# Packed attention and SwiGLU on one core: early packed weights at their final scale in PSUM, and a new order of all engines

## The chip, the cores and the metric

The kernel runs on 1 core of one Trainium2 chip. The metric is the device time of one execution in microseconds (us); the time of the kernel before is the median of 3 runs. A profile is one execution taken by the hardware profiler. Its engines are PE (TensorE, matmuls), PEld (its weight loads), DVE (VectorE), ACT (ScalarE), POOL (GpSimd) and SP (SyncE, which here issues all transfers).

## The reference

```python
# q, k, v: (8, 8, 576, 64); p: (8, 8, 32, 64); scale = 1 / sqrt(64)
def sm_attn(qq, kk, vv):
    s = scale * np.matmul(qq, kk.transpose(0, 1, 3, 2))
    s = s - np.max(s, axis=-1, keepdims=True)
    a = np.exp(s)
    a = a / (np.sum(a, axis=-1, keepdims=True) + 1e-09)
    return np.matmul(a, vv)
p_packed = sm_attn(p, k, v)              # 32 packed rows per head
out = sm_attn(q, p_packed, p_packed)
# x: (4608, 512), the heads side by side; d_ff = 1536
xn = x / np.sqrt(np.mean(x * x, axis=-1, keepdims=True) + 1e-06) * rms_g
g = xn @ w_gate
return (g / (1 + np.exp(-g)) * (xn @ w_val)) @ w_out
```

The three weights arrive as 64-bit floating point numbers, as pairs of 32-bit words.

## The kernel before

**What is computed, and in which pieces.** The second attention multiplies its weights `a` with the packed rows, and the result goes through `w_gate` and `w_val`. The kernel therefore multiplies the packed rows with these weights once per batch ("packed weights", `packed_weights`, L1138): for each of 6 column groups `c` a matmul group on the fp32 weights `wgv` (L1172) into two PSUM banks, which `pw_evict` (L1212) splits into two fp16 parts in `ring`. From batch 3 on (`PW16_FROM`) the weights have themselves been split into fp16 (`weights16`, L1192) and the matmuls are those of L1184. The tokens go through in 12 units of 384 (`u`). For each there is `query` (loading and transposing q), `attention` (scores L1357 or L1364, softmax, norm, and the attention transposed in `aTu`) and the MLP: the up projection, 24 groups of L1549, with `gated` (SiLU, product, split into two fp16 parts in `hall`), and the down projection, three outputs of 36 matmuls each (L1574), with `store`. `keysets` and `stage1` do the first attention of a batch. Units 0 and 1 and batches 0 and 1 ("early") work in fp32 on PE.

**The front.** The 12 pieces of `w_gate` and `w_val` (`gv_piece`, L581) and 6 of `w_out` (`wo_piece`) are 1 MB each and go through nine raw rooms that are used again. `to_f32` (L540) makes fp32 of them: ACT takes the high halves (L548); the low halves go by a letter of `LOW` or `LOW_WO`: "D" two DVE operations (L563, L565), "A" one of ACT (L558) and one of DVE (L560), "P" one of POOL (L553) and one of DVE (L555). A norm of each pair of pieces (L618 on PE, reduced over 512 columns at L623) gives its scale `gv_r` and the value half's factor `ratio` (L631). When all norms are there, `wo_split` splits `w_out` (ACT L707, DVE L709, and a copy by ACT, L715, or POOL, L712, by a letter of `WO_HI`); the down projection of unit 0 needs it.

**Scales.** In batches 0 to 2 the gate half is multiplied with `pg` itself and the value half with `pg` times `ratio` (L1157, L1159; the engine by `PGV_BY`); the eviction then scales by the column `gv_r`:

```python
yield from split(hi, lo, ps[e], pw_sc[:, c : c + 1] if b < PW16_FROM else 2.0**-14, 512, t0, DVE)
```

`split` is an ACT activation with a scale (L513) and a DVE `scalar_tensor_tensor` (L515), which takes the high part away.

**What sets the order.** The functions are generators that ask a planner (`Plan`) for a room or for an engine with a cost in us. The planner runs them against its own clock and writes the order of every engine's queue, which the chip then follows. Which step goes first is set by `RANK`, `BUMP`, `LATER`, `CHOICE` and `AGE`, tables with one entry per phase; `SLACK` holds PE steps outside the MLP back; `KEYS_AFTER` says behind which weight load the keys of batch 1 are let go. Letters as in `KEYS_BY`, `QUERY_BY`, `A1T_BY`, `H_HI` and `H_LO` name the engine that copies. Where PE would wait in the front, `fill` puts in matmuls on constants ("fillers", L1656, 256 columns).

Of the kernel before, what the change touches and what calls it, by code (L numbers as in the profile page):

```python
# [18 lines left out]
P = 128  # L19
# [15 lines left out]
LATENCY = {PE: 0.299, ACT: 0.177, EXP: 0.177, SILU: 0.177, DVE: 0.14, DVE2: 0.14, POOL: 0.005}  # L35
# [12 lines left out]
AGE = (0.106, 0.001, 0.011, 0.097, 0.0, 0.0, 0.486)  # L48
# [5 lines left out]
WINDOW, DENSE = 3.41, 0.47  # L54

# [36 lines left out]
class Plan:  # L92
# [104 lines left out]
    def start(self, chain):  # L197
        kind, _, *at = chain.ask[:3]
        e = ENGINE[kind]
        if at and at[0] is not None:  # L200
# [4 lines left out]
        t = float(ready)
        if e == "pe" and chain.key[0] != "mlp":
            t += SLACK[self.phase]
        free = self.free[e] + (TABLE if kind in (EXP, SILU) and kind != self.table else 0.0)
        return max(free, t), ready
# [18 lines left out]

    def fill(self, until, matmul):

        begin = self.free["pe"]
        if self.stage or until > FILL[2] or until - begin < FILL[0]:
            return
        spare = [(r[0], n, name) for name in ("pm", "psc") for n, r in enumerate(self.rooms[name])]
        if len(self.rooms["pa"]) == 2:
            spare.append((max(r[0] for r in self.rooms["pa"]), 0, "pa"))
        spare = [x for x in spare if x[0] <= max(0.0, begin - FILL[4])]
        unit = 0.213 if self.slow(begin) else 0.125
# [8 lines left out]
        self.free["pe"] += unit * count  # L247
        self.rooms[name][n] = (t, room)

    def run(self, matmul):  # L250
        while self.chains:
            self.settle()
            steps = [c for c in self.chains if c.ask is not None and c.ask[0] in ENGINE]
            if not steps:
                assert not self.chains, [(c.key, c.ask) for c in self.chains]
                return
            starts = []
            for c in steps:
                t, ready = self.start(c)
                t -= AGE[self.phase] * max(0.0, t - ready)  # L260
                starts.append((t, self.precedence(c), c))
            first = min(starts, key=lambda s: s[:2])
            e = ENGINE[first[2].ask[0]]
            window = CHOICE[self.phase][e]
            chain = min(
                (s for s in starts if ENGINE[s[2].ask[0]] == e and s[0] <= first[0] + window), key=lambda s: (s[1], s[0])
            )[2]
            t, ready = self.start(chain)
            kind, cost, *_ = chain.ask
            if e == "pe":  # L270
                self.fill(t, matmul)
                t = max(t, self.free["pe"])
            if kind == LOAD:
                self.free[e] = t + 0.45
                self.landed = max(self.landed, t + LOADING[0]) + cost / LOADING[1]
                seen = self.landed + LOADING[2]
            elif kind == TPOSE:
                issue = 0.1 + cost / 786432 * 3.5
                self.free[e] = t + issue
                self.landed = max(self.landed + 0.9 * issue, t + issue)  # L280
                seen = self.landed + TURNING
            else:
                if kind in (EXP, SILU) and kind != self.table:
# [17 lines left out]
RANK = ({'attention': 0.0, 'conv': 34.24, 'g': 13.88, 'gated': 0.0, 'keys': 0.0, 'mlp': 1000000000.0, 'pw': 7.98, 'pw_evict': 8.66, 'query': 0.0, 'scales': 15.65, 'stage1': 2.05, 'store': 16.88, 'v': 9.6, 'w': 23.15, 'wo': 10.17, 'wo_split': 40.04}, {'attention': 81.35, 'conv': 17.08, 'g': 20.02, 'gated': 9.94, 'keys': 8.3, 'mlp': 1000000000.0, 'pw': 3.23, 'pw_evict': 1.17, 'query': 5.95, 'scales': 4.48, 'stage1': 17.4, 'store': 12.51, 'v': 30.41, 'w': 10.59, 'wo': 4.57, 'wo_split': 14.41}, {'attention': 23.62, 'conv': 32.67, 'g': 28.29, 'gated': 0.0, 'keys': 14.43, 'mlp': 1000000000.0, 'pw': 4.11, 'pw_evict': 3.27, 'query': 4.57, 'scales': 3.23, 'stage1': 0.0, 'store': 0.0, 'v': 7.35, 'w': 31.34, 'wo': 21.47, 'wo_split': 11.2}, {'attention': 22.8, 'conv': 8.01, 'g': 30.57, 'gated': 0.0, 'keys': 0.0, 'mlp': 1000000000.0, 'pw': 6.0, 'pw_evict': 7.89, 'query': 9.74, 'scales': 0.0, 'stage1': 10.65, 'store': 22.96, 'v': 14.82, 'w': 0.37, 'wo': 2.3, 'wo_split': 14.0}, {'attention': 25.03, 'conv': 2.72, 'g': 6.23, 'gated': 5.32, 'keys': 18.98, 'mlp': 1000000000.0, 'pw': 21.74, 'pw_evict': 1.05, 'query': 10.61, 'scales': 5.16, 'stage1': 24.79, 'store': 4.96, 'v': 8.99, 'w': 9.01, 'wo': 1.31, 'wo_split': 6.69}, {'attention': 17.8, 'conv': 0.0, 'g': 7.83, 'gated': 8.05, 'keys': 15.4, 'mlp': 1000000000.0, 'pw': 0.0, 'pw_evict': 3.38, 'query': 27.04, 'scales': 4.68, 'stage1': 19.89, 'store': 10.11, 'v': 56.26, 'w': 22.66, 'wo': 18.33, 'wo_split': 0.0}, {'attention': 0.59, 'conv': 16.59, 'g': 22.57, 'gated': 10.43, 'keys': 46.12, 'mlp': 1000000000.0, 'pw': 5.64, 'pw_evict': 0.0, 'query': 16.98, 'scales': 26.73, 'stage1': 34.01, 'store': 6.52, 'v': 23.39, 'w': 15.29, 'wo': 27.47, 'wo_split': 7.09})  # L301
# [13 lines left out]
KV_LOAD = (1.05, 0.95)  # L315
# [1393 lines left out]
```

## Time and profile before

| what | value |
| --- | --- |
| median of 3 runs | 752.8 us (751.02 to 755.01) |
| profiled execution | 753.8 us; span from first to last instruction 751.7 us |
| PE, DVE, ACT, POOL busy | 727.1, 484.5, 461.6, 124.0 us |
| mean granted clock of PE | 0.99 of full |
| transfers | 82.31 MB |

A busy PE also holds its fillers and matmuls at a lower granted clock, so its 97% is not useful work alone. Idle time of an engine that sets nothing costs nothing.

### The profile page before, as it was taken

To read this page: it belongs to the slowest core of one execution; us is meant where nothing else is said; L and a number is where in the kernel's file an instruction comes from. 1 tells how busy PE (TensorE), PEld (TensorE's weight loads), DVE (VectorE), ACT (ScalarE), POOL (GpSimd) and SP (SyncE) were. 2 spreads that over 40 slices of the span, in tenths; PEclk is the share of its full clock that TensorE was granted. 3 is DMA by queue.
4 is the path that set the end of the run, shared out by engine and by line. 5 is a ranking of instruction groups with operands and counts; after the bars stand their busy time and mean duration, and the time that the engine had idled before them with its cause. 6 is when DMAs were issued, how large, how long until landed. Compare 5 with 4: busy or idle time off the path is not lost.

```text
span 751.7 us, 20141 instructions
## 1 busy us (share of the span) xinstructions
PE 727.1 (97%) x8537; PEld 439.8 (59%) x8537; DVE 484.5 (64%) x1084; ACT 461.6 (61%) x959; POOL 124.0 (17%) x138
## 2 busy tenths in 40 slices
PE   8889999999999999999999999999989999999997
PEld 6765655875555554585555464685544464684553
DVE  4899797875896886777576555586447463572330
ACT  3597796886787676586387376587366274371330
POOL 1213230020342242121011011010001011010010
PEclk9899999999999999999999999999999999999999
DMA  8998413355366165424724923363321213301001
GB/s 291 386 313 303 152 33 79 77 143 140 81 142 133 45 149 150 75 64 80 175 66 79 204 68 104 80 122 102 90 43 23 71 37 98 72 3 43 21 1 43
DMA packets 131418, 82.31 MB, mean 109 GB/s; under 512 B 98432, under 2 KB 110720, under 8 KB 131328
## 3 DMA queue, kind: packets, MB, share of 16 engines
q1 hardware_dynamic: 131328, 81.02, 41.5%
q8 instruction: 67, 1.10, 0.6%
q14 instruction: 23, 0.19, 0.1%
HBM read 47.97 MB, written 9.44 MB: 76 GB/s over the span
## 4 chain that ended last, share of the span: by engine, by line
PE 79%; DMA 6%; ACT 6%; DVE 5%; issue 2%; SPq 1%; POOL 0%; ACTq 0%; DVEq 0%; POOLq 0%
PE pm_2x L1574 10%; PE pm_0x L1574 9%; PE pm_1x L1549 9%; PE pm_2x L1549 9%; PE pm_1x L1574 8%; PE pm_3x L1549 8%; PE pm_3x L1574 7%; PE pm_0x L1549 7%; DMA ring<-in_moe_w_val_dram 2%; DMA wo<-in_moe_w_val_dram 2%; PE psa L1364 2%; PE psb L1017 2%; PE pm_3x L1184 1%; DMA big_1x<-big_5x 1%; PE psa L923 1%
## 5 line engine op out<-in xcount | busy, mean ns | idle before, releaser
L1549 PEld LDWEIGHTS <-ring 128*128 128x128 f16 x2304 | 204.9, 98 | 91.9 <-issue 20.6
L1574 PEld LDWEIGHTS <-hall 128*128 128x128 f16 x1296 | 123.4, 98 | 149.3 <-issue 9.0
L1574 PE MATMUL pm_2x<-wo,hall 128*128 128x512 f16 x360 | 81.4, 379 | 2.1 <-ACT wo L715 1.2
L1603 POOL TENSOR_TENSOR hall<-t_0x,hall 128x384 f16<-128x384 f32 x36 | 36.3, 1007 | 285.0 <-ACT hall L1600 275.7
L1574 PE MATMUL pm_0x<-wo,hall 128*128 128x512 f16 x360 | 81.0, 379 | 0.0
L1574 PE MATMUL pm_3x<-wo,hall 128*128 128x512 f16 x288 | 65.9, 379 | 0.0
L1574 PE MATMUL pm_1x<-wo,hall 128*128 128x512 f16 x288 | 64.5, 379 | 0.0
L1600 ACT CAST hall<-t_1x 128x384 f16<-128x384 f32 x71 | 36.2, 509 | 26.5 <-DVE t_1x L1586 26.1
L1603 POOL TENSOR_TENSOR hall<-t_1x,hall 128x384 f16<-128x384 f32 x29 | 28.9, 998 | 134.2 <-ACT hall L1600 125.7
L1549 PE MATMUL pm_3x<-aTu_0x,ring 128*128 128x192 f16 (+1 forms) x330 | 45.8, 282 | 1.5 <-DVE ring L515 1.2
L1549 PE MATMUL pm_1x<-aTu_0x,ring 128*128 128x384 f16 (+1 forms) x306 | 45.4, 292 | 0.4 <-DVE ring L515 0.4
L1549 PE MATMUL pm_2x<-aTu_1x,ring 128*128 128x192 f16 (+1 forms) x324 | 45.8, 285 | 0.0
L1549 PE MATMUL pm_1x<-aTu_1x,ring 128*128 128x192 f16 (+1 forms) x330 | 44.7, 279 | 0.9 <-ACT t_0x L1583 0.8
L1600 ACT CAST hall<-t_0x 128x384 f16<-128x384 f32 x67 | 34.1, 509 | 17.4 <-DVE t_0x L1586 17.1
L1549 PE MATMUL pm_2x<-aTu_0x,ring 128*128 128x192 f16 (+1 forms) x288 | 41.1, 287 | 0.7 <-ACT t_1x L1583 0.6
L1549 PE MATMUL pm_3x<-aTu_1x,ring 128*128 128x384 f16 (+1 forms) x258 | 37.7, 289 | 0.0
L1549 PE MATMUL pm_0x<-aTu_1x,ring 128*128 128x384 f16 (+1 forms) x240 | 36.6, 294 | 0.0
L1549 PE MATMUL pm_0x<-aTu_0x,ring 128*128 128x384 f16 (+1 forms) x228 | 34.3, 292 | 1.0 <-DVE ring L515 0.5
L1606 DVE TENSOR_TENSOR hall<-t_1x,hall 128x384 f16<-128x384 f32 x44 | 24.5, 557 | 6.6 <-ACT hall L1600 5.9
L1583 ACT ACT_TABLE_LOAD x15 | 19.2, 1283 | 8.9 <-PE pm_1x L1549 5.3
L1583 ACT ACTIVATE t_0x<-pm_0x,usc_1x 128x384 f32<-128x384 f32 x14 | 8.1, 579 | 26.8 <-PE pm_0x L1549 26.7
L1606 DVE TENSOR_TENSOR hall<-t_0x,hall 128x384 f16<-128x384 f32 x35 | 20.8, 594 | 5.2 <-ACT hall L1600 5.0
(972 smaller groups left out, 1405.8 us busy)
## 6 DMA issues: line engine op xcount, KB each, us to landing
out_dram<-o_1x SPq DMA_DIRECT2D x19, 256.0 KB, 2.0
out_dram<-o_0x SPq DMA_DIRECT2D x17, 256.0 KB, 2.2
hall<-in_moe_w_out_dram SPq DMA_DIRECT2D x4, 1024.0 KB, 6.5
wo<-in_moe_w_gate_dram SPq DMA_DIRECT2D x3, 1024.0 KB, 15.3
wo<-in_moe_w_val_dram SPq DMA_DIRECT2D x3, 1024.0 KB, 13.5
big_2x<-in_k_dram SPq DMA_DIRECT2D x5, 576.0 KB, 5.5
big_1x<-in_q_dram SPq DMA_DIRECT2D x3, 768.0 KB, 6.0
ring<-in_moe_w_gate_dram SPq DMA_DIRECT2D x2, 1024.0 KB, 13.2
```

The costliest lines, as they stand in the source:

```text
L923: nc.tensor.matmul(flat[r, KP * c0 : KP * c1], pT[:, 2 * g + hl, r], kTs[j // 2][1][:, n + c0 : n + c1, q], start=(hl == 0), stop=(hl == 1),)
L1017: nc.tensor.matmul(pps[g][32 * j : 32 * j + 32, :D], a1T[h, c, 32 * j : 32 * j + 32], half(vf0[b, j // 2])[h, j % 2, order[c], :], start=( ...
L1184: nc.tensor.matmul(ps[e][32 * j : 32 * j + 32, :], pg[h, lp, j, :], wgv16[h, c, j, lw, :], start=(n3 == 0), stop=(n3 == 2),)
L1364: nc.tensor.matmul(ps2[o : o + n, i, :, pi, :], qT[:, lq, i, pi, o : o + n], packs[b][3][:, lp, pi, :, :], start=(j == 0), stop=(j == 2),)
L1549: nc.tensor.matmul(psi[:, :, o : o + n], pw[:, g, lw, w, f * P : (f + 1) * P], aT[:, :, la, g, o : o + n], start=(j == 0), stop=(j == 5),)
L1574: nc.tensor.matmul(po, hall[:, ft, lh, ts], wo[:, ft, 1 - lw, :], start=(n == 0), stop=(n == 3 * NFT - 1))
L1583: nc.scalar.activation(t, pss[0][:, :UT], AF.Silu, scale=sc[:, c, 0:1])
L1600: nc.scalar.copy(hall[:, ft, 0, :], t)
L1603: nc.gpsimd.tensor_tensor(hall[:, ft, 1, :], t, hall[:, ft, 0, :], ALU.subtract)
L1606: nc.vector.tensor_tensor(hall[:, ft, 1, :], t, hall[:, ft, 0, :], ALU.subtract)
```

## The change

Four edits change what is computed where, and one the order of everything:

1. `packed_weights` of batches 0 to 2 multiplies `pg` with both columns of `gv_r` before the matmuls (two ACT activations, or one DVE or POOL operation over 256 columns), and the eviction scales by the constant 1.0. `ratio` and `vg_sc` go.
2. The norm of a pair of weights adds both column halves in one PSUM range; L623 reduces 256 columns.
3. Four small operations of `load_g` go from DVE to POOL. Fillers have 512 columns.
4. The letters that name engines are new, and `KEYS_AFTER` is 10.
5. The planner charges PE for a change between matmuls on part of the array and on the whole (`SWITCH`) and for the fetch of PE's instructions, counted by the matmul (`FETCH`); costs, ranks and the other tables are new. Branches for splitting in other ways are added, which the letters chosen (`LO_BY`, `SPLIT_BY`, `MUL_BY`) leave unused.

The core of the diff:

```diff
-SLACK = (0.04, 0.166, 0.039, 0.236, 0.337, 0.234, 0.47)
+SLACK = (0.081, 0.203, 0.691, 0.758, 0.387, 0.765, 0.246)
+SWITCH = 0.093
+FETCH = (4.3, 6.3, 8.0)
+FETCH_AT, FETCH_NEED, FETCH_SIZE = 128, 449, 256
...
+    def fetched(self, t, cost, n):
+        a, b = self.count, self.count + 2 * n
+        self.count = b
+        late = 0.0
+        for k in range(max(0, (a - FETCH_NEED) // FETCH_SIZE), b // FETCH_SIZE + 1):
+            for at in (FETCH_SIZE * k + FETCH_AT, FETCH_SIZE * (k - 1) + FETCH_NEED):
+                if not a <= at < b:
+                    continue
+                x = t + late + cost * (at - a) / (b - a)
+                if at == FETCH_SIZE * k + FETCH_AT:
+                    self.avail[k] = x + FETCH[0 if self.landed <= x else 2 if self.stage == 0 and x < 90 else 1]
+                else:
+                    late += max(0.0, self.avail.get(k - 1, 0.0) - x)
+        return cost + late
...
-A1T_BY = "DAADAD"
+A1T_BY = "DDDDAD"
-PGV_BY = "DAPAAA"
-GM_BY = "ADDADD"
-LOW = "DDPDDDAAADDA"
-LOW_WO = "DPAPDP"
-KEYS_AFTER = 13
-KEYS_BY = "DDDAAADDDAAD"
-QUERY_BY = "DDADAA"
-H_HI = "DDAADAADADAD"
-H_LO = "PDPDPPPDDPDP"
-H_LO_MIXED = "DDDDDPDPDPPD"
-H_LO_ONE = "PPDDDDPDPPPD"
+PGV_BY = "DAPAAP"
+GM_BY = "AADADA"
+LOW = "ADPAAAADAPAP"
+LOW_WO = "APAPDP"
+KEYS_AFTER = 10
+KEYS_BY = "DAADADDDDADA"
+QUERY_BY = "AAADDA"
+H_HI = "DADDDAADDDAD"
+H_LO = "DPDDPDDPDPPP"
+H_LO_MIXED = "DPDPPDPDPDDD"
+H_LO_ONE = "PDPDPPPPPDDD"
-GV_BY = "PPDDPP"
-WO_HI = "AAPPAP"
+GV_BY = "PDDDPP"
+WO_HI = "AAAAAP"
...
-                        pn[:, (2 * w + f) * P : (2 * w + f + 1) * P], r, r, start=(kt == 0), stop=(kt == NKT - 1)
+                        pn[:, w * P : (w + 1) * P], r, r, start=(f + kt == 0), stop=(f == 1 and kt == NKT - 1)
-        nc.vector.tensor_reduce(mx, pn.rearrange("p (w f) -> p w f", w=2), AX.X, ALU.max)
+        nc.vector.tensor_reduce(mx, pn[:, : 2 * P].rearrange("p (w f) -> p w f", w=2), AX.X, ALU.max)
-        nc.vector.tensor_scalar(ratio[:, c : c + 1], u[:, 0:1], s[:, 1:2], 0.5, ALU.mult, ALU.mult)
...
-                    nc.scalar.activation(pgs[1], pg, AF.Copy, scale=ratio[:, c : c + 1])
+                    for w in range(2):
+                        nc.scalar.activation(pgs[:, w], pg, AF.Copy, scale=gv_r[:, c, w : w + 1])
                 else:
-                    (nc.vector if by == "D" else nc.gpsimd).tensor_scalar_mul(pgs[1], pg, ratio[:, c : c + 1])
+                    (nc.vector if by == "D" else nc.gpsimd).tensor_tensor(
+                        pgs.rearrange("p w j r -> p w (j r)"),
+                        pg.rearrange("p j r -> p (j r)").unsqueeze(1).broadcast_to([P, 2, P]),
+                        gv_r[:, c].unsqueeze(2).broadcast_to([P, 2, P]), ALU.mult,
+                    )
...
-            yield from split(hi, lo, ps[e], pw_sc[:, c : c + 1] if b < PW16_FROM else 2.0**-14, 512, t0, DVE)
+                yield from split(hi, lo, ps[e], 1.0 if b < PW16_FROM else 2.0**-14, 512, t0, DVE)
...
-        nc.tensor.matmul(room[:, 0, :256] if len(room.shape) == 3 else room[:, :256], margin, fill, start=True, stop=True)
+        nc.tensor.matmul(room[:, 0, :512] if len(room.shape) == 3 else room[:, :512], margin, fill, start=True, stop=True)
```

## Rows read from the trace of the kernel before

**Rows 1.** Windows: length, busy us of each engine, clock, DMA share, GB/s.

```profile
20.00:54.00 34.00, 28.35 (x326) 21.79 (x323) 31.60 (x67) 25.07 (x45) 6.95 (x9) 0.85 1.06 344
54.00:110.00 56.00, 51.83 (x684) 33.97 (x684) 50.25 (x100) 46.16 (x76) 18.29 (x19) 1.00 0.52 181
110.00:160.00 50.00, 49.69 (x745) 34.29 (x744) 39.81 (x94) 36.84 (x86) 4.99 (x6) 1.00 0.40 92
160.00:735.00 575.00, 566.89 (x6416) 330.50 (x6414) 353.10 (x799) 345.76 (x741) 90.99 (x90) 1.00 0.37 86
735.00:752.00 17.00, 12.76 (x60) 5.59 (x57) 1.24 (x2) 0.47 (x1) 0.00 (x0) 0.95 0.08 32
```

**Rows 2.** The chain that ended last, the front: start, us, what.

```profile
7.17 14.12 DMA ring<-in_moe_w_val_dram
...
22.97 5.10 PE psa L1357 x24
...
40.67 13.49 DMA wo<-in_moe_w_val_dram
...
103.07 1.24 POOL wo L712
...
108.47 1.05 ACT wo L715
...
109.56 2.53 PE pm_2x L1574 x11
```

**Rows 3.** Waits of PE: who waited for whom, total us, times, longest.

```profile
PE psa L1441 <- issue: 2.1, 1, 2.1
PE psa L1357 <- DVE misc L1056: 2.1, 1, 2.1
...
PE pm_2x L1574 <- ACT wo L715: 1.2, 1, 1.2
...
PE psa L923 <- DMA big_5x<-big_1x: 1.0, 1, 1.0
PE pm_2x L1574 <- issue: 0.9, 1, 0.9
...
PE psa L1364 <- DMA big_1x<-big_5x: 0.8, 1, 0.8
```

**Rows 4.** PE alone while L1357 ran: window, busy, clock, DMA share, GB/s.

```profile
23.00:28.00 5.00, 5.00 (x26) 0.53 1.05 386
```

**Rows 5.** Timeline of DVE: start, us, line, operation, tiles.

```profile
30.56 0.68 DVE L623 TENSOR_REDUCE tiny_11x<-pm_3x 128x2 f32<-128x512 f32 x1
31.16 0.69 DVE L563 TENSOR_SCALAR wgv<-wgv 128x1024 uint32<-128x1024 uint32 x1
...
34.76 0.21 DVE L631 TENSOR_SCALAR ratio<-tiny_12x,gv_r 128x1 f32<-128x1 f32 x1
34.89 1.22 DVE L565 SCALAR_TENSOR_TENSOR wgv<-wo,wgv 128x1024 uint32<-128x1024 uint32 x1
...
37.95 0.42 DVE L1252 TENSOR_SCALAR aT_0x<-psb 128x256 f32<-128x256 f32 x1
38.29 1.22 DVE L565 SCALAR_TENSOR_TENSOR wgv<-wo,wgv 128x1024 uint32<-128x1024 uint32 x1
```

**Rows 6.** Evictions into `ring`, ACT and DVE: count, ns min/median/max, starts, form.

```profile
L513 ACT ACTIVATE ring<-pm_0x x19: 577/592/602, 249.4 to 670.8; 128x512 f16<-128x512 f32 x19
...
L513 ACT ACTIVATE ring<-pm_0x,gv_r x7: 663/680/706, 66.2 to 208.2; 128x512 f16<-128x512 f32 x7
...
L515 DVE SCALAR_TENSOR_TENSOR ring<-pm_0x,ring x19: 680/682/692, 250.1 to 671.4; 128x512 f16<-128x512 f32 x19
...
L515 DVE SCALAR_TENSOR_TENSOR ring<-pm_1x,gv_r,ring x11: 736/743/751, 40.6 to 221.7; 128x512 f16<-128x512 f32 x11
```

**Rows 7.** Two ACT operations of the front, columns as in rows 6.

```profile
L558 ACT ACTIVATE hall<-hall x3: 1123/1146/1199, 38.6 to 65.1; 128x1024 uint32<-128x1024 uint8 x3
...
L1157 ACT ACTIVATE pgh_1x<-pg_0x,ratio x3: 398/401/402, 46.2 to 72.1; 128x128 f32<-128x128 f32 x3
```

More of the change, by code (lines that the diff above doesn't have):

```diff
@@ L26 @@
 DVE2 = "dve2"
+PET = "pet"
 EXP, SILU = "exp", "silu"
-ENGINE = {PE: "pe", ACT: "act", EXP: "act", SILU: "act", DVE: "dve", DVE2: "dve", POOL: "pool", LOAD: "sp", TPOSE: "sp"}
+ENGINE = {PE: "pe", PET: "pe", ACT: "act", EXP: "act", SILU: "act", DVE: "dve", DVE2: "dve", POOL: "pool", LOAD: "sp", TPOSE: "sp"}
 ENGINES = (
@@ L208, in start @@
         free = self.free[e] + (TABLE if kind in (EXP, SILU) and kind != self.table else 0.0)
+        if kind == PET and not self.tiled:
+            free += SWITCH
         return max(free, t), ready
@@ L237, in fill @@
         spare = [x for x in spare if x[0] <= max(0.0, begin - FILL[4])]
-        unit = 0.213 if self.slow(begin) else 0.125
+        unit = 0.42 if self.slow(begin) else 0.232
         count = int((FILL[1] * (until - begin) - FILL[3]) / unit)
@@ L246, in fill @@
         self.work.append((begin, begin + unit * count, 1.0))
-        self.free["pe"] += unit * count
+        self.free["pe"] += self.fetched(begin, unit * count, count)
+        self.tiled = False
         self.rooms[name][n] = (t, room)
@@ L307 @@
+LATER = {'attention': 78.44, 'conv': -63.68, 'g': -131.85, 'gated': 45.4, 'keys': 72.7, 'pw': 1.66, 'pw_evict': -105.25, 'query': 18.16, 'scales': -18.72, 'stage1': -12.53, 'store': 16.97, 'v': 32.7, 'w': 23.17, 'wo': -135.91, 'wo_split': 125.94}
 RAW_AT = (0, 1, 2, 3, 4, 5, 6, 7, 8, 4, 5, 6)
@@ L409, in upper @@
         return x.bitcast(BF16)[..., 1::2]
-    misc = cpool.tile([P, 640], F32, name="misc")
-    fill = misc[:, 512:640].bitcast(BF16)
+    misc = cpool.tile([P, 768], F32, name="misc")
+    fill = misc[:, 512:768].bitcast(BF16)
     nc.gpsimd.memset(fill, 0.0)
+    minus = fill.bitcast(F16)[:, :P]
+    nc.gpsimd.tensor_scalar_mul(minus, ident, -1.0)
     neghalf = cpool.tile([P, 1], F32, name="neghalf")
@@ L430, in tile_packed_attention_then_swiglu @@
     gv_r = cpool.tile([P, NFC, 2], F32, name="gv_r")
-    pw_sc = gv_r[:, :, 0]
-    ratio = cpool.tile([P, NFC], F32, name="ratio")
-    vg_sc = cpool.tile([P, NFC], F32, name="vg_sc")
     wo_sc = cpool.tile([P, NFC], F32, name="wo_sc")
@@ L703, in wo_split @@
         x, sc = wo32[:, 2 * i : 2 * i + 2, :], wo_sc[:, i : i + 1]
+        if SPLIT_BY[i] == "H":
+            for f in range(2):
+                st = yield Room("o")
+                k = 2 * i + f
+                hi, lo = wo[:, k, 1, :], wo[:, k, 0, :]
+                yield (ACT, act(512) + 0.03) if SPLIT_ST[k] == "A" else (DVE2, 0.37)
+                if SPLIT_ST[k] == "A":
+                    nc.scalar.activation(st, wo32[:, k], AF.Copy, scale=sc)
+                else:
+                    nc.vector.tensor_scalar_mul(st, wo32[:, k], sc)
+                yield (ACT, act(512)) if HALF_HI[k] == "A" else (DVE, 0.34)
+                (nc.scalar.copy if HALF_HI[k] == "A" else nc.vector.tensor_copy)(hi, st)
+                if SPLIT_LO[k] == "P":
+                    yield POOL, 1.17
+                    nc.gpsimd.tensor_tensor(lo, st, hi, ALU.subtract)
+                else:
+                    yield DVE2, dve(512) + 0.1
+                    nc.vector.tensor_tensor(lo, st, hi, ALU.subtract)
+                plan.give("o", st)
+            plan.mark("wo_hl", i)
+            return
         hi0 = yield Room("o")
         hi = hi0.bitcast(F16).rearrange("p (f n) -> p f n", f=2)
-        yield ACT, act(1024)
+        yield ACT, act(1024) + 0.06
         nc.scalar.activation(hi, x, AF.Copy, scale=sc)
@@ L811, in keys32 @@
                 by = KEYS_BY[6 * b + 3 * w + i]
-                yield (ACT, act(n * P)) if by == "A" else (DVE, dve(n * P))
+                yield (ACT, act(n * P) - 0.06) if by == "A" else (DVE, dve(n * P) + 0.035)
                 (nc.scalar.copy if by == "A" else nc.vector.tensor_copy)(dst, pm[rows, : n * P])
@@ L935, in scores @@
                 plan.mark("scored", b)
-            yield DVE, dve(576) + 0.45
+            yield DVE, dve(576) + (0.29 if early else 0.44)
             if not early:
@@ L972, in evict @@
             n = (c1 - c0) * P
-            yield (ACT, act(n), t) if by == "A" else (DVE, dve(n) + 0.05, t)
+            yield (ACT, act(n) - 0.05, t) if by == "A" else (DVE, dve(n) + 0.03, t)
             (nc.scalar.copy if by == "A" else nc.vector.tensor_copy)(a1T0[:, c0 * P : c1 * P], pat)
@@ L1054, in stage1 @@
                 h = slice(64 * g, 64 * g + 64)
-                yield (DVE, dve(64), t_t) if g else (ACT, act(64), t_t)
+                yield (DVE, 0.32, t_t) if g else (ACT, 0.25, t_t)
                 (nc.vector.tensor_copy if g else nc.scalar.copy)(pb32[b][h, :, g, :], ptx[h])
@@ L1091, in stage1 @@
         if (b + 1) * S > EARLY * UT:
-            yield ACT, 2 * act(128) + 0.22, t_t
+            yield ACT, 2 * act(128) + (0.42 if early else 0.22), t_t
             for g in range(2):
@@ L1197, in weights16 @@
             st = yield Room("o")
-            if c + k == 0:
-                yield DVE, 0.2
-                nc.vector.scalar_tensor_tensor(vg_sc, pw_sc, 0.5, ratio, ALU.mult, ALU.mult)
             yield DVE2, dve(512) * 0.7 + 0.14
-            for w, sc in enumerate((pw_sc, vg_sc)):
+            for w in range(2):
                 n = slice(2 * P * w, 2 * P * (w + 1))
-                nc.vector.tensor_scalar(st[:, n], x[:, n], sc[:, c : c + 1], 1.0 if w else 0.5, ALU.mult, ALU.mult)
+                nc.vector.tensor_scalar(st[:, n], x[:, n], gv_r[:, c, w : w + 1], 0.5, ALU.mult, ALU.mult)
             yield ACT, act(512)
@@ L1216, in pw_evict @@
             hi, lo = (t[:, e, l].rearrange("p w f -> p (w f)") for l in range(2))
-            yield from split(hi, lo, ps[e], pw_sc[:, c : c + 1] if b < PW16_FROM else 2.0**-14, 512, t0, DVE)
+            if b == 0 and LO_BY[2 * c + e] == "A":
+                yield ACT, act(512) - 0.045, t0
+                nc.scalar.copy(hi, ps[e])
+                yield PE, pe(512, 1), plan.now, 1.0, 1
+                nc.tensor.matmul(ps[e], minus, hi, start=False, stop=True, skip_group_check=True)
+                yield ACT, act(512) - 0.045
+                nc.scalar.copy(lo, ps[e])
+            else:
+                yield from split(hi, lo, ps[e], 1.0 if b < PW16_FROM else 2.0**-14, 512, t0, DVE)
             plan.give(*held[e])
@@ L1322, in query @@
                 yield from split(
-                    *(qhl[:, l, i].rearrange("s (h d) -> s h d", h=H) for l in range(2)), q_[:, :, i, :], sq, 580, t
+                    *(qhl[:, l, i].rearrange("s (h d) -> s h d", h=H) for l in range(2)), q_[:, :, i, :], sq, 515, t
                 )
@@ L1373, in attention @@
         ri = yield Room("t24")
-        yield DVE, 2 * dve(768) + 0.42
+        yield DVE, 2 * dve(768) + (0.25 if early else 0.42)
         for b, r, o, n in parts(u):
```

144 lines of the change are left out of this document (79 added, 65 removed).

## Prediction

> **What bounds the kernel now.** I read the windows of the trace first [rows 1]. From 54 us on, TensorE (PE) is the bound: it is busy 51.8 of 56 us up to 110, 49.7 of 50 up to 160 and 566.9 of 575 up to 735. The last 17 us hold 4.2 idle, the end of the last store. So after 54 us PE waits 4.2 + 0.3 + 8.1 = 12.6 us besides that tail, and no reordering can take more than this out of the part that is 93% of the span. What is left is how early PE gets work without gaps. Between 20 and 54 us PE is busy 28.4 of 34 us, part of it with the planner's filler matmuls, while VectorE (DVE) is busy 31.6 of 34 (93%) and the DMA engines are full (share 1.06, 344 GB/s).
>
> The chain of work that ended last, read in order of time, agrees [rows 2]: two long pieces of the front are DMA (14.12 us from 7.17, 13.49 us from 40.67, both weight loads), with attention of unit 0 on PE in between (5.10 us). At the end of the front stand the splits of `w_out`: a POOL copy of 1.24 us at 103.07, then ACT work, then an ACT copy of 1.05 us at 108.47, for which PE stood 1.2 us [rows 3] before the down projection went on at 109.56. From there the chain is almost PE alone.
>
> The waits of PE [rows 3] show how little is to be had later: the longest single ones are 2.1 and 0.9 us of "issue" (no engine was waited for), and 1.0 us for a transposing DMA. In the front it stood 2.1 us for a DVE copy (L1056), and then ran the scores of unit 0 at half its clock [rows 4].
>
> **The change part by part.** Costs on a busy engine are from one start to the next, because neighbours overlap [rows 5]: a DVE operation over 512 columns (L623, 0.68 long) gives way after 0.60, one over 256 (L1252, 0.42 long) after 0.34, a one-column one (L631, 0.21 long) after 0.13.
>
> *DVE.* (a) LOW and LOW_WO name fewer conversions "D": 7 of 12 become 2, and 2 of 6 become 1. Each saves the shift L563, as long (0.69) as the L623 before it, so 0.60: 6 x 0.60 = 3.6 us. (b) The norm of a weight pair is summed into 256 columns in place of 512, so L623 falls from 0.60 to 0.34: 6 x 0.26 = 1.6 us. (c) `ratio` goes: 6 x 0.13 = 0.8 us. (d) Evictions L515 of batches 0 to 2 take a constant. The trace has both forms, 0.743 with `gv_r` and 0.682 without [rows 6]; 12 of the 36 fall into the front: 12 x 0.06 = 0.7 us. (e) The hand-over lists move work in: two copies of a1T, two casts and one subtraction of `hall` (384 columns, bounded by 0.34 and 0.60, taken at 0.47) are 2.35 us, one query copy leaves (0.60), three small operations more and two 128-column reductions less about cancel (-0.2), and the one DVE scaling of `pg`, now 256 columns wide, is at most 0.34 dearer, taken at 0.1: together +1.6. Sum: -3.6 - 1.6 - 0.8 - 0.7 + 1.6 = -5.1 us. By the starts of the present instructions, some 3.9 of this lies before 54 us (four of six L563, four of six L623 and `ratio`, four evictions) and 1.2 behind.
>
> *ACT.* It takes over four more low halves (L558, 1.15 us each [rows 7], 4.6), two more `w_out` copies (1.05 [rows 2], 2.1), and for `pg` six scalings where there were four (0.40 [rows 7], so +0.8); the evictions give back 12 x 0.088 = 1.1 (0.680 against 0.592 [rows 6]); of what is handed over, one query copy and two small reductions come and two a1T copies and two casts go, between 0 and two copies of 0.592, taken at -0.5. Together +5.9 us. ACT is idle 9 us of 34 before 54 us and 10 of 56 behind it [rows 1], and that idle time is the cover; without it the 5.9 us would undo the DVE's 5.1.
>
> *POOL.* Two low halves more and one wider `pg` scaling more against two copies L712 and a few small operations less: near zero in an engine busy 25 of 90 us. The gain is the place of L712: it stood on the chain.
>
> *PE.* The matmuls on fp32 weights (L1172) and the norm matmuls stay in number and size: 0. Fillers of 512 columns in place of 256 only fill waits: 0, between a coarser filler that delays the next matmul and one that keeps the clock up; neither has a row, and one matmul of delay is inside the range.
>
> *SP.* The keys of batch 1 are let go after weight load 10 and not 13. That puts 1.2 MB ahead of the last loads, 3.4 us at the 344 GB/s of [rows 1]. I take 0, because before 54 us the loads wait for rooms that conversions set free (the 13.49 us load was issued at 40.67, right behind a conversion on the chain), and keep 3.4 as a bound.
>
> **The sum, as time of PE.** First term, the front before 54 us: the first up projection of unit 0 can come earlier by what DVE loses, 3.9 us, if DMA lets it. Bounds 0 (DMA is full there) and -6.4 (if the 2.1 us wait also shrinks until the 5.10 us piece runs at full clock, half of that is saved as well). I take -3.0, nearer the row that shows DVE 93% busy. Second term, 54 to 110: PE idles 4.2 us, of which 1.2 is the wait behind the copy; bounds 0 and -4.2, taken -2.0. Third term, 110 to 735: PE idles 8.4 us, and 3.0 of that are the two "issue" waits, which the new planner charges for by counting matmuls; bounds -4 and +16 (below), taken -1.5. The Trainium skill speaks against this third term: "Runtime: NRT & Kernel Launch", section Instruction fetch mechanics, says that crossing a block of 256 instructions is mostly hidden. By that rule the third term would be 0 and the time 1.5 us longer; the rows show that 3 us are not hidden.
>
> The profiled execution took 753.8 us (span 751.7), 1.0 above the median of 752.8. 753.8 - 3.0 - 2.0 - 1.5 = 747.3, and less 1.0 for the median 746.3: I say **746**.
>
> **Rivals.** What a measurement of this kernel can tell from no change is about 0.5%, 3.8 us: faster is under 749, slower over 756.6.
>
> *No change: DMA holds the front.* The DMA share of 1.06 speaks for it: all weights must be in before the last split, and quicker conversions then only wait for data. Against it: the share falls to 0.52 after 54 us. First term 0, second -1, third 0: 752.8 - 1 = 751.8. If the keys' 3.4 us come on top, 755.2.
>
> *A much better front.* The whole list is drawn anew, so PE may get what it idles: -6.4 before 54, -4.2 behind, -3 later: 753.8 - 13.6 - 1.0 = 739. For it: ACT and DVE together have 27 us free between 20 and 110. Against it: no single edit frees that much.
>
> *Slower: attention comes late in every unit.* The new order holds PE's other steps back longer (SLACK up to 0.77 us where it was 0.47 at most) and hands PE's time to the MLP. If the chain query, scores, transposition of a later unit ends behind the MLP that covers it, PE stands at L923 and L1364. It does so now once each, 1.0 and 0.8 us [rows 3]. In ten units that is 18 - 1.8 = +16 us: 753.8 - 5.0 + 16 - 1.0 = 764. It decides from some 9 us of such waits on. Against it: between 160 and 735 DVE is 61% and ACT 60% busy, so there is room.
>
> A constant of 1.0 that costs as much as the pointer would take 0.7 us back on DVE and 1.1 on ACT, less than can be told.
>
> **How the numbers follow.** Forecast (742 to 749) 0.48; better front 0.15; no change 0.24; late attention 0.13. Faster: 0.48 + 0.15, less 0.01 at the edge, 0.62. Same: 0.24 + 0.01 = 0.25. Slower 0.13. The range 738 to 755 holds the forecast, most of the better front and the no-change case; outside it stay the slow case and the best of the good one.
>
> **What would show it.** In the changed profile: evictions of early batches at 0.59 and 0.68 us; three shifts L563 in place of nine and reductions near 0.42 us; the first up projection before 51 us; the POOL copy gone from the chain; the down projection of unit 0 running without a break before 107; PE's idle time between 160 and 735 at or below 8 us. The prediction is wrong if the first up projection stays at 53 us with DMA in front of it (no change), or if PE's idle time in that long stretch goes beyond 15 us (slower).

## The result, and the profile after

The changed kernel took **746.4 us** (median of 5 runs, 745.4 to 747.7), the kernel before 753.1 beside it: a ratio of 0.991 with an interval of 0.988 to 0.993. The forecast was 746, faster. Run again as it is, it gave 0.992 (0.990 to 0.994). A second run of the unchanged kernel before gave 1.002 (1.001 to 1.003) against itself, so 0.2% (1.5 us) between two medians says nothing.

The windows of the changed kernel, columns as in [rows 1]:

```profile
20.00:54.00 34.00, 27.35 (x451) 20.70 (x455) 27.83 (x65) 25.06 (x49) 5.52 (x7) 0.80 1.07 334
54.00:110.00 56.00, 50.02 (x671) 31.83 (x671) 51.70 (x104) 50.76 (x89) 19.68 (x18) 1.00 0.53 191
110.00:160.00 50.00, 49.15 (x732) 35.44 (x731) 38.44 (x90) 37.14 (x87) 8.33 (x9) 1.00 0.41 92
160.00:735.00 575.00, 570.33 (x6431) 331.21 (x6429) 349.30 (x786) 336.33 (x732) 100.01 (x99) 1.00 0.38 86
735.00:744.00 9.00, 4.73 (x22) 1.95 (x20) 0.48 (x1) 0.47 (x1) 0.00 (x0) 0.89 0.08 29
```

DVE has 3.8 us less to do between 20 and 54 us, as worked out ahead (3.9). PE's busy time there falls by 1.0 us, but fillers were 6.40 us of it before and are 1.57 us now, so PE's other work in this window grew by 3.8 us. In the row that is 575 us long its idle time is 4.7 us in place of 8.1. The chain of the front, as in [rows 2]:

```profile
11.34 10.38 DMA big_4x<-in_v_dram
...
26.71 3.60 PE psa L1424 x24
...
101.40 1.21 DVE wo L766
102.63 1.04 ACT wo L772
...
107.86 0.94 ACT wo L772
108.85 2.75 PE pm_1x L1644 x12
```

The POOL copy of `w_out` is gone from the chain, and the scores of unit 0 take 3.60 us where they took 5.10. But an ACT copy stands where the POOL copy was, another one still stands ahead of PE, and the last 12 matmuls of the down projection's first output begin at 108.85, only 0.7 earlier. PE's waits, as in [rows 3]:

```profile
PE psb L1074 <- issue: 2.7, 2, 2.5
PE pm_3x L1619 <- DVE ring L550: 1.5, 1, 1.5
...
PE psa L1431 <- DMA big_2x<-big_0x: 0.9, 1, 0.9
PE pm_1x L1619 <- ACT t_1x L1653: 0.8, 1, 0.8
```

**A boundary with the same work on both sides.** A window cut at a fixed time mixes work that another order has put earlier or later. The down projection of unit 0 ends on the same matmul in every kernel here, and behind it every kernel runs the same 6,922 matmuls up to the last down matmul. The timeline of PE gives both ends. Kernel before:

```profile
133.65 1.24 PE L1574 MATMUL pm_0x<-wo,hall 128*128 128x512 f16 x5
...
746.74 1.03 PE L1574 MATMUL pm_2x<-wo,hall 128*128 128x512 f16 x4
```

Changed kernel:

```profile
130.75 1.24 PE L1644 MATMUL pm_1x<-wo,hall 128*128 128x512 f16 x5
...
738.71 1.03 PE L1644 MATMUL pm_3x<-wo,hall 128*128 128x512 f16 x4
```

So the front ends at 133.65 + 1.24 = 134.9 before and at 132.0 after (-2.9), and the long part takes 746.74 + 1.03 - 134.89 = 612.9 before and 607.7 after (-5.2). All profiles, read in this way (idle: PE's gaps of over 0.1 us in the long part, summed; stall: the longest wait called issue that has no engine behind it, from 20 us on):

```
kernel                       median  ratio (interval)        front  long    idle  stall
before                       753.1   -                       134.9  612.9    7.9  2.1 at 549
before, again       (e9)     754.5   1.002 (1.001-1.003)     136.5  611.9    6.8  2.1 at 550
changed                      746.4   0.991 (0.988-0.993)     132.0  607.7    5.3  2.5 at 356
changed, again      (e5)     747.6   0.992 (0.990-0.994)     134.3  607.7    5.5  2.2 at 358
old order, new arith (e1)    752.0   0.998 (0.996-0.999)     136.8  610.1    7.3  2.5 at 550
new order, old arith (e2)    749.4   0.994 (0.992-0.996)     134.5  608.1    5.9  2.4 at 358
LOW undone          (e6)     750.4   0.997 (0.995-0.999)     135.1  607.5    5.2  2.5 at 359
both reliefs undone (e10)    752.8   1.000 (0.998-1.001)     138.4  608.3    6.1  2.2 at 362
+64 from the start  (e3)     745.9   0.990 (0.988-0.992)     135.2  605.1    2.6  1.5 at 26
+128 from the start (e4)     747.9   0.993 (0.991-0.994)     138.3  604.0    1.9  3.3 at 24
+64 at 58 us        (e11)    743.4   0.987 (0.985-0.989)     132.4  605.3    3.0  0.5
+128 at 58 us       (e12)    745.2   0.989 (0.987-0.991)     136.5  604.6    2.6  0.4
old order, wide fillers (e8) 758.3   1.007 (1.005-1.010)     134.8  616.0   10.7  4.2 at 547
no charges          (e7)     799.2   1.061 (1.059-1.063)     145.9  649.9   31.2  0.4
```

Two profiles of one kernel agree to 1.0 us or better in the long part; in the front they differ by 1.6 and 2.3. So a front that only one profile shows is known to some 2 us.

### The profile page after: what moved, and what is told of

It reads as the page before. It is cut to its first block, busy times and chain, and to the rows that moved or that the text cites. A ratio compares the mean times of both kernels' runs of the same rounds, so it can differ in the third digit from the quotient of the medians.

```text
span 743.6 us, 19963 instructions
## 1 busy us (share of the span) xinstructions
PE 717.0 (96%) x8447; PEld 430.7 (58%) x8452; DVE 475.5 (64%) x1061; ACT 458.1 (62%) x966; POOL 138.0 (19%) x153
## 4 chain that ended last, share of the span: by engine, by line
PE 80%; ACT 7%; DVE 5%; DMA 4%; issue 2%; SPq 1%; POOL 1%; DVEq 0%; ACTq 0%; POOLq 0%
PE pm_3x L1644 10%; PE pm_3x L1619 9%; PE pm_1x L1644 9%; PE pm_2x L1619 8%; PE pm_1x L1619 8%; PE pm_0x L1644 8%; PE pm_2x L1644 8%; PE pm_0x L1619 7%; PE psb L1074 2%; PE psa L1431 2%; DMA big_4x<-in_v_dram 1%; PE pm_0x L1246 1%; PE psa L980 1%; DMA big_2x<-big_0x 1%; DMA big_5x<-big_2x 1%
## 5 line engine op out<-in xcount | busy, mean ns | idle before, releaser
L1619 PEld LDWEIGHTS <-ring 128*128 128x128 f16 x2304 | 204.2, 98 | 90.4 <-issue 18.7
L1673 POOL TENSOR_TENSOR hall<-t_1x,hall 128x384 f16<-128x384 f32 x46 | 46.8, 1017 | 244.4 <-ACT hall L1670 231.9
L1644 PE MATMUL pm_3x<-wo,hall 128*128 128x512 f16 x360 | 80.9, 379 | 0.0
L1644 PE MATMUL pm_1x<-wo,hall 128*128 128x512 f16 x324 | 73.7, 379 | 0.2 <-ACT wo L772 0.2
L1644 PE MATMUL pm_0x<-wo,hall 128*128 128x512 f16 x324 | 73.4, 379 | 0.0
L1644 PE MATMUL pm_2x<-wo,hall 128*128 128x512 f16 x288 | 65.1, 379 | 0.0
L1619 PE MATMUL pm_3x<-aTu_0x,ring 128*128 128x192 f16 (+1 forms) x360 | 49.3, 281 | 1.5 <-DVE ring L550 1.5
L1619 PE MATMUL pm_3x<-aTu_1x,ring 128*128 128x384 f16 (+1 forms) x312 | 44.7, 286 | 0.0
L1619 PE MATMUL pm_2x<-aTu_1x,ring 128*128 128x192 f16 (+1 forms) x312 | 43.5, 283 | 0.1
L1619 PE MATMUL pm_2x<-aTu_0x,ring 128*128 128x384 f16 (+1 forms) x276 | 40.1, 288 | 1.3 <-ACT t_0x L1653 1.3
L1619 PE MATMUL pm_1x<-aTu_0x,ring 128*128 128x384 f16 (+1 forms) x282 | 41.2, 289 | 0.0
L1619 PE MATMUL pm_1x<-aTu_1x,ring 128*128 128x384 f16 (+1 forms) x258 | 37.8, 289 | 1.4 <-ACT t_1x L1653 0.8
L1619 PE MATMUL pm_0x<-aTu_1x,ring 128*128 128x384 f16 (+1 forms) x270 | 38.9, 287 | 0.0
L1619 PE MATMUL pm_0x<-aTu_0x,ring 128*128 128x384 f16 (+1 forms) x234 | 34.5, 289 | 0.8 <-DVE t_1x L1656 0.4
L1653 ACT ACTIVATE t_1x<-pm_2x,usc_1x 128x384 f32<-128x384 f32 x13 | 7.5, 576 | 27.8 <-issue 22.7
L1267 POOL TENSOR_TENSOR wgv<-o_1x,wgv 128x512 f16<-128x512 f32 x11 | 13.9, 1267 | 51.3 <-ACT wgv L1265 51.3
L1267 POOL TENSOR_TENSOR wgv<-o_0x,wgv 128x512 f16<-128x512 f32 x13 | 15.5, 1196 | 42.6 <-ACT wgv L1265 42.6
```

The costliest lines, as they stand in the source:

```text
L1267: nc.gpsimd.tensor_tensor(wgv16[:, c, k, 1], st, wgv16[:, c, k, 0], ALU.subtract)
L1619: nc.tensor.matmul(psi[:, :, o : o + n], pw[:, g, lw, w, f * P : (f + 1) * P], aT[:, :, la, g, o : o + n], start=(j == 0), stop=(j == 5),)
L1644: nc.tensor.matmul(po, hall[:, ft, lh, ts], wo[:, ft, 1 - lw, :], start=(n == 0), stop=(n == 3 * NFT - 1))
L1653: nc.scalar.activation(t, pss[0][:, :UT], AF.Silu, scale=sc[:, c, 0:1])
L1673: nc.gpsimd.tensor_tensor(hall[:, ft, 1, :], t, hall[:, ft, 0, :], ALU.subtract)
```

## The experiments

**Which edits make the gain: order or arithmetic.** Old order with the new arithmetic (e1), new order with the old arithmetic (e2), the first on the kernel before, the second the reverse on the changed one; the edit in short:

```diff
-pgs = [pg, room...]; pgs[1] = pg * ratio;  split(hi, lo, ps[e], pw_sc[:, c : c + 1], ...)   # norm in 512 columns
+pgs = room...;       pgs[w] = pg * gv_r[w]; split(hi, lo, ps[e], 1.0, ...)                   # norm in 256 columns
```

> The order, the lists and the planner's costs of the kernel before, instruction for instruction, with only the arithmetic of the change: the packed weights' norm reduced over 256 columns, no ratio, both halves of pg scaled, early evictions by 1.0. Order theory (the gain is PE's time after 110 us, and comes from where the new order lays its matmuls; the cheaper arithmetic hides): 752 to 753 us, at most 1 us under before; evictions L515 of the early batches at 0.68 us and reductions near 0.42 us, but PE's time after 110 us as before. Front theory (what DVE loses in the front, 1.6 + 0.8 + 0.7 = 3.1 us, is what makes the kernel faster): 749.5 to 750.5 us.

> The order, the lists and the planner's costs of the changed kernel, with the arithmetic of before: ratio, evictions by a pointer's scale, norm reduced over 512 columns, one half of pg scaled. Order theory: 746 to 747 us, the whole gain is kept, with evictions at 0.74 us again. Front theory: about 3 us dearer than the changed kernel, 749 to 750 us. If both this run and the one with the old order stand between the two kernels, the two parts add.

Measured: the arithmetic alone gives 1.8 us (0.998), the order with the old arithmetic 4.5 (0.994). Both stand between the two kernels, so neither theory holds alone and the parts add: 1.8 + 4.5 = 6.3. But the share of the arithmetic is barely clear of noise: the unchanged kernel gave 1.002 against itself, and e2's interval (0.992 to 0.996) overlaps that of the changed kernel run again (0.990 to 0.994). Nor does e1's profile show it in the front, which ends at 136.8; from 20 us on 17.1 us of that front ran at half clock, against 10.2 in both profiles of the kernel before. e1's long part is shorter (610.1 against 612.9 and 611.9), and there the clock did not fall behind the stall. In e1 all 12 early evictions on DVE are at 0.68 us and the reductions at 0.42, from its groups by line:

```profile
L515 DVE SCALAR_TENSOR_TENSOR ring<-pm_1x,ring 128x512 f16<-128x512 f32 x5 | 3.4, 687 | 0.3 <-ACT ring L513 0.2
...
L623 DVE TENSOR_REDUCE tiny_13x<-pm_2x 128x2 f32<-128x256 f32 x1 | 0.4, 418 | 0.0
```

**The low halves.** The changed kernel's order, but `LOW` and `LOW_WO` carried out as before (e6):

```diff
+LOW_DONE = "DDPDDDAAADDA"; LOW_WO_DONE = "DPAPDP"   # the old lists, for what is executed
-    yield from to_f32(x, raw, 1024, LOW[i])
+    yield from to_f32(x, raw, 1024, LOW[i], None, LOW_DONE[i])
```

> The changed kernel's order, with the low halves LOW and LOW_WO carried out on the engines of before: five of the twelve weight conversions and one of the six of w_out go back to the DVE shift, 6 x 0.60 = 3.6 us more of DVE in the front and as many low halves less on ACT. Front theory: this was the largest term of the forecast, so 2 to 3.6 us slower than the changed kernel, 748.5 to 750. Cover theory (before 54 us PE waits for the loads and for ACT, not for DVE's sum): at most 1 us slower, 746 to 747.4.

Measured 750.4 beside 747.6 for the changed kernel (e5), 0.997 against 0.992: 2.8 us by the medians, 3.8 by the ratios. The front theory's 2 to 3.6 holds by the medians, and the cover theory falls: this relief of DVE is on the path. The long part stays at 607.5.

**Both reliefs undone (e10)**, the two edits above together:

> The changed kernel's order with both the arithmetic and the low halves of before: only the order, the hand-over lists and the wide fillers are left of the change. If the two reliefs add (each alone undone: 749.4 against 747, and 750.4 against 747.6), 2.4 + 2.8 = 5.2 us dearer than the changed kernel, 751.5 to 753: the order alone is then worth next to nothing, since its front loses about what its long part gains. If they do not add: 749.5 to 751. From the end of unit 0 to the last down matmul 607 to 608.5 us in either case, as in the changed kernel.

Measured 752.8 beside 752.7 for the kernel before: with the old arithmetic and the old low halves, the new order is worth nothing. It was laid for the cheaper operations, though, and the old order with both reliefs was not run; so this does not tell an order that is dear in itself from one that fits only its own costs. The reliefs add: against 0.9912, the mean of the changed kernel's two ratios, undoing the arithmetic costs 0.28%, the low halves 0.56%, and both 0.84% (6.3 us). The profile says how nothing comes about: the long part keeps its gain (608.3), and the front ends at 138.4, 2.7 us later than the mean of the two profiles of the old order (135.7) and 5.3 later than that of the two of the changed kernel (133.1). PE's waits show where: between 20 us and the end of the front it waits 12.6 us for DVE in e10 (sum of its waits over 0.1 us) and 12.3 in e6, against 6.6 and 8.4 in the two profiles of the changed kernel. The clock explains little of that difference: from 20 us on it was at half for 13.7 us of the front in e10, for 13.7 and 10.2 in the changed kernel, and for 6.8 in e6. In e10 two stretches at half clock lie where PE has nothing but work:

```profile
63.40:66.80 3.40, 3.40 (x38) 1.17 (x36) 2.54 (x4) 2.45 (x3) 1.01 (x1) 0.50 0.91 344
87.30:90.70 3.40, 3.40 (x19) 2.34 (x18) 2.95 (x6) 2.13 (x5) 3.00 (x2) 0.50 1.07 331
```

At half clock these 6.8 us did 3.4 us of work.

**The place in PE's instruction stream.** The changed kernel with its first eight fillers given as 5 (e3) or 9 (e4) narrow matmuls each:

```diff
+if len(narrow) < 8 and len(room.shape) == 2:
+    narrow.append(room)
+    for _ in range(5):                        # e4: 9, of 48 columns
+        nc.tensor.matmul(room[:32, :96], margin[:, :32], fill[:, 256 : 256 + 96], start=True, stop=True)
+    return
```

> The changed kernel, with its first eight fillers each given as five narrow matmuls (128x32 weights, 96 columns) in place of one of 512 columns: about as long in columns, and 32 matmuls, so with their weight loads 64 instructions of PE, more. All that follows on PE is 64 instructions later in its stream, in the same order. Phase theory (a part of PE's stalls called issue stands at fixed places of the instruction stream, every 256 instructions, and the new order lays work there that hides them): the stalls move to other work, so PE's issue waits after 110 us rise by some us, from 42 towards the 49 of before, and the time by 2 to 6 us, to 748 to 752. Front theory and the theory that only the order counts and not its place in the stream: 746 to 747 us, and the issue waits as in the changed kernel.

> As the run above, but each of the first eight fillers as nine matmuls of 48 columns: 64 matmuls, 128 instructions of PE, more. Phase theory: the stalls fall half a period away from where the new order was laid for them, the time rises by 2 to 8 us, to 748 to 754, and differs from that of the 64-instruction shift. Both other theories: 746 to 747 us.

No theory's expectation held in full. The issue waits named there (42 and 49 us) are those of the weight loads after 110 us (waits over 0.15 us); they stay at 41.5 and 41.9, so the phase theory's rise did not come. The times (745.9, 747.9) hardly move, but both parts do: the long part falls to 605.1 and 604.0, where its stall of 2.5 us is gone, and the front ends at 135.2, within what two profiles differ by, and at 138.3. In e4 a stall of 3.3 us stands in the front, and the scores of unit 0 run at half clock behind it, its waits and windows of PE:

```profile
PE psb L1074 <- issue: 3.3, 1, 3.3
```

```profile
23.50:26.80 3.30, 0.03 (x3) 0.00 (x0) 0.00 (x0) 0.00 (x0) 1.09 (x1) 0.50 1.05 388
26.80:36.00 9.20, 8.57 (x55) 7.51 (x55) 4.12 (x15) 5.21 (x10) 1.72 (x3) 0.50 1.05 386
```

So the stall does hang on the place in the stream, but the order had not been laid around it: either shift is better in the long part.

**What repeats.** Both kernels once more, nothing edited:

> The changed kernel once more, nothing edited, as a measure of what one profile says. All theories: 746 to 747 us. The place theory (a long issue stall belongs to a place of PE's instruction stream): the 2.5 us stall at the attention value matmuls of unit 3, at about 355 us, is there again within some 10 matmuls. If long stalls are chance, it is somewhere else or nowhere. From the end of unit 0 (its last down matmul) to the last down matmul the profile should again show 607 to 608 us, against 612.9 before.

> The kernel before once more, nothing edited, as a measure of what one profile says: 752.5 to 754. Place theory: the 2.1 us issue stall is there again at the attention matmuls of unit 8, at about 549 us, within some 10 matmuls of its place in PE's stream; whether the clock falls behind it may differ. From the end of unit 0 to the last down matmul 610 to 613 us. Chance theory: that stall is elsewhere or gone.

The place theory holds in both, though both times lie 0.5 to 0.6 us above what was expected (747.6 and 754.5). Counted in PE's records, the stall of the changed kernel stands behind the 4,556th matmul in both profiles and in e6, that of the kernel before behind the 6,864th in both. Also the clock fell behind it both times; windows of the kernel before, first the profile shown ahead, then the second:

```profile
549.27:551.38 2.11, 0.00 (x1) 0.00 (x0) 0.68 (x2) 0.51 (x1) 0.00 (x0) 1.00 0.01 4
552.40:555.80 3.40, 3.40 (x12) 1.64 (x11) 0.62 (x1) 2.09 (x10) 0.00 (x0) 0.50 0.03 7
```

```profile
552.40:556.00 3.60, 3.60 (x14) 1.69 (x13) 0.20 (x1) 2.44 (x11) 0.00 (x0) 0.54 0.03 7
```

**The fillers of the old order (e8)**, paired into 512 columns:

```diff
-for _ in range(count):
-    matmul(room)
+for k in range(0, count, 2):
+    matmul(room, 512 if k + 1 < count else 256)
```

> The kernel before, with its fillers paired into 512 columns: 53 matmuls, 106 instructions of PE, fewer ahead of all that follows; order and arithmetic as before. Place theory: the 2.1 us stall in unit 8 at 549 us, and the 3.4 us at half clock that followed it in that profile, fall elsewhere or vanish: from the end of unit 0 to the last down matmul 612.9 becomes 608 to 611, and the time 750 to 752 unless the front pays. Forecast's own term (fillers count for nothing): 753 to 754.

The front is the same (134.8), the long part 616.0, and the time 758.3: 0.7% (5 us) worse than before and outside both expectations. The stalls did move, but to worse places: 2.5 us at 269 and 4.2 at 547, and the clock was at half for twice as long, from within the second on:

```profile
PE pm_2x L1549 <- issue: 4.2, 1, 4.2
PE psb L1441 <- issue: 2.5, 1, 2.5
```

```profile
549.50:556.30 6.80, 4.79 (x84) 2.52 (x84) 0.62 (x1) 0.93 (x2) 0.00 (x0) 0.50 0.01 3
```

**The planner's charges (e7):**

```diff
-SWITCH = 0.093
+SWITCH = 0.0
-                    late += max(0.0, self.avail.get(k - 1, 0.0) - x)
-        return cost + late
+                    late = 0.0
+        return cost
```

> The lists and the arithmetic of the changed kernel, planned without the charges for an instruction block that arrives late and for a switch of PE's work, so the order is another one. Planner theory (the charges make the order good in the long part): 2 to 5 us slower, 748.5 to 751.5, with more issue waits of PE after 135 us. Chance theory (orders differ, and the charges find nothing that is real): within 2 us of the changed kernel on either side, 744.5 to 748.5.

799 us, far outside both. In part it is the "attention late" rival of the prediction come true: of the 31.2 us of idle PE, 14.1 are waits of up projections for the transposed attention (`aTu`), and the rest is mostly for `t` (SiLU and product) and `ring` (packed weights). The longest waits of PE from 135 us on:

```profile
PE pm_1x L1619 <- ACT t_1x L1653: 6.0, 2, 3.0
PE pm_3x L1619 <- DVE ring L550: 4.8, 3, 3.9
PE pm_2x L1619 <- DMA aTu_1x<-hl_0x: 4.4, 1, 4.4
PE pm_3x L1619 <- DMA aTu_1x<-hl_0x: 3.6, 1, 3.6
```

Issue waits, which the planner theory expected to grow, were 0.2 us in the long part. The run says nothing on what the charges are worth: ranks and bumps that fit one cost model may give a poor order under another, and no run separates the two. It shows how far an order can go wrong: 31 us of idle PE, and seven falls of the clock behind 135 us.

**A version that beats both (e11, e12).** 32 or 64 small matmuls in the wait of 1.5 us that PE has ahead of the second up projection of unit 0 (the L1619 row of the waits above):

```diff
+if u + ft == 0 and w == 1:
+    for _ in range(32):                       # e12: 64
+        nc.tensor.matmul(ps[:32, :16], margin[:, :32], fill[:, 256:272], start=True, stop=True)
```

> The changed kernel with 32 matmuls of 16 columns (64 instructions of PE) more, into a room that the second up projection of unit 0 overwrites, in the wait of 1.5 us that PE has there at 58 us. The front up to there stays as it is, and all that follows is 64 instructions later in the stream. Place theory: the 2.2 to 2.5 us stall at 355 us goes, as in the run that had this shift from the start (605.1 us from the end of unit 0 on, against 607.7), and the front is not disturbed: 743.5 to 745. Other theories: 746.5 to 748.

> The same with 64 matmuls, 128 instructions. Place theory: 604 us from the end of unit 0 on, as in the run that had this shift from the start, so 742.5 to 744.5, less what the longer row of small matmuls stands out of the wait, 0 to 1 us. Other theories: 746.5 to 748.5.

With 32 the time is 743.4, a ratio of 0.987 (0.985 to 0.989), the best of all; its five executions (741.5 to 744.8) all lie under the eleven of the changed kernel (745.0 to 748.6). The front is left as it was (132.4) and the long part takes 605.3. The longest waits of PE from 135 us on are now

```profile
PE pm_1x L1622 <- ACT t_1x L1656: 0.8, 1, 0.8
PE pm_1x L1622 <- ACT t_0x L1656: 0.5, 1, 0.5
...
PE pm_0x L1647 <- issue: 0.5, 1, 0.5
```

With 64 the long part is 604.6, as expected, but the front of its profile ends at 136.5 (17.1 us of it from 20 us on at half clock, against 10.2 with 32), and the time is 745.2, at the upper end of what was expected and not clear of the changed kernel's.

## Why the prediction came out right

The total (746, measured 746.4) was right; its terms were not. Two errors nearly cancel, so it is luck that the total came so close.

**The front, first and second term: too large.** Taken together -5.0 us; measured to the end of unit 0's down projection -2.9 in the profiles shown, and -2.6 between the means of two profiles each. The relief of DVE was well sized. What e10 undoes was forecast at 6.7 us (3.6 + 1.6 + 0.8 + 0.7; the 1.6 us handed over to DVE stay in e10), and undoing it costs 5.3 us in the front and 6.3 by the ratios. Its parts: arithmetic 3.1 forecast, 1.8 (e1) to 2.1 measured; low halves 3.6 forecast, 2.8 to 3.8 measured. DVE's busy time from 20 us to the end of the front agrees: 101.0 us before, 94.4 after, 101.0 again in e10, so the 1.6 us handed over do not show in it. Of the 3.9 us that were put before 54 us, the listed parts add up to 4.2; the profile shows 3.8.

The step that failed is what stood at 0: the order itself ("SP: I take 0" and PE "0"). Without the reliefs, the front under the new order is 2.7 us dearer than under the old one by e10's profile; by the times it is some 3.8, since e10 takes as long as the kernel before while its long part is 4.1 us shorter. The marker failed with it: the first up projection of unit 0 was to come before 51 us. PE's timeline, the kernel before and then the changed one:

```profile
52.99 1.14 PE L1549 MATMUL pm_0x<-aTu_0x,ring 128*128 128x384 f16 x6 [0.47 <-DVE tiny_21x L497]
```

```profile
56.79 1.33 PE L1619 MATMUL pm_0x<-aTu_0x,ring 128*128 128x384 f16 x6
```

It comes at 56.8 (58.3 in the second profile). The new order runs all three groups of unit 1's query transposes (L1361, the last at 52.39) ahead of it, the old one only one. What makes the front dearer is not settled. One candidate is ACT, whose idle time was to be the cover. In the profile shown, the chain that ended last is ACT alone from 33.17 to 46.4 us:

```profile
33.17 1.13 ACT wo L595
34.30 0.48 ACT ring L548
34.77 1.02 ACT wgv L585
...
45.35 1.03 ACT hall L595
```

In the second profile the chain from 20 to 54 us is mostly DMA (16.2 us), but from 54 to 110 us the chain holds 22.9 and 23.3 us of ACT in the two profiles, against 16.7 and 7.3 before. Another candidate is the last weight load, issued at 40.67 before [rows 2], which now goes out at 49.54, behind `p` and the keys of batch 1. A third is the clock: e10 ran 13.7 us at half clock from 20 us on, the kernel before 10.2. No run moved these loads alone, or took work off ACT alone.

**The long part, third term: too small.** -1.5 forecast, -5.2 measured, and -4.7 between the means of two profiles, beyond its bound of -4. The term was made from PE's idle time, and above all from the issue waits that the planner was to lay elsewhere. Idle fell by 2.0 (7.4 to 5.4, means), but the issue waits only by 0.6 (3.4 and 2.9 before, 2.5 and 2.6 after): a stall of 2.5 us took the place of the one of 2.1. The rest is work that got shorter. Up projections, each counted up to the start of the next matmul, take 266.7 us in both profiles of before and 264.2 to 264.5 in all with the new order but e7; 0.9 of the 2.5 is idle and some 1.6 are the 3.4 us at half clock behind the stall at 549. A busy PE at half clock isn't in a count of idle time, and a window of 575 us rounds it to 1.00 [rows 1]. The same 264.2 stands in e1, which has the old order and its stall, but no fall of the clock there; so this part of the gain is not the order's alone. About 1 us is left over, spread over lines.

**The rule against the third term.** By the Trainium skill, "Runtime: NRT & Kernel Launch", section Instruction fetch mechanics, crossing a block is mostly hidden, and the third term would have been 0. The trace agrees for most: 54 instruction packets of 16 KB are fetched after 135 us, and in either kernel one stall of over 2 us stands there. If that stall is such a crossing, as the times of the packets below suggest, it is not small: 2.1 us and some 1.6 of clock before, 2.5 after, and moving it is worth 2.4 us of the long part (e11). The prediction's "the rows show that 3 us are not hidden" went too far: its second wait, of 0.9 us, was 0.5 in the second profile.

**The rivals.** No change: against it stands e6, since DVE's time before 110 us does pay, DMA full or not. Late attention did not come; PE's waits for transposes of later units were 1.0 + 0.8 us before [rows 3] and 0.9 + 0.5 after (0.9 + 0.6 and 0.8 + 0.6 in the second profiles). Of the signs named: evictions at 0.59 and 0.68, three shifts, no POOL copy on the chain, and 4.7 us of idle (at most 8) were right; the first up projection before 51, and a down projection unbroken before 107 (broken until 108.85), were wrong.

## What to carry to other kernels

Cut a trace at an instruction that all versions share, with the same work on either side, before a gain is put down to a stage; a cut at a time put some of this gain in the wrong place. Look at the clock in short windows behind a long stall: behind 2.1 us of stall PE lost some 1.6 us more here, while busy. When a stall of PE has no engine behind it and comes back at the same instruction, shift the stream by some dozens of small matmuls put into an existing wait, and measure: one of the four shifts here paid 0.4% (e11), the other three 0.2% or nothing.

## What was not expected of the hardware

Each of the stalls of 1.9 to 4.2 us called issue, in ten profiles, stands within a run of short attention matmuls or a few matmuls behind one (24 at most). The timeline of the changed kernel, PE:

```profile
355.40 0.23 PE L1074 MATMUL psb<-big_1x,a1T_0x 64*32 64x64 f32 x2
358.10 0.30 PE L1074 MATMUL psb<-big_1x,a1T_0x 64*32 64x64 f32 x4 [2.47 <-issue]
```

and its windows, ahead of the stall and in it:

```profile
353.99:355.63 1.64, 1.64 (x141) 1.48 (x140) 0.00 (x0) 0.00 (x0) 0.00 (x0) 1.00 1.12 212
355.63:358.10 2.47, 0.00 (x2) 0.01 (x1) 0.00 (x0) 0.00 (x0) 0.00 (x0) 1.00 0.69 44
```

PE used up 141 matmuls and 140 weight loads in 1.64 us, about 6 ns for each instruction, while the DMA engines were full with transposes and a store (share 1.12). An instruction packet starts at 355.6, as the stall begins, and the next one at 359.1; in the kernel before packets start at 548.6 and 552.6 around its stall. It looks as if a run of short matmuls eats its instructions faster than the next block comes. That the stall belongs to a place in the stream is shown (e3, e4, e5, e9, e11); that it is a fetch is argued from the packets' times. Full queues are not needed for it: the DMA share within the stall is 0.01 in both profiles of the kernel before and 0.00 in both stalls of e1. Open is also why the clock fell behind 2.1 us of stall in both profiles of the kernel before, and not behind 2.2 to 2.5 us in five profiles with the new order, nor in e1.
